# Where the weight sums of a two-level product scheme are staged and which engine makes them

## The chip, the cores and the metric

The kernel runs on one core of one Trainium2 chip. A core has a matrix engine (TensorE, PE in the profile, with its weight loads as PEld), a vector engine (VectorE, DVE), a scalar engine (ScalarE, ACT), a general engine (GpSimd, POOL) and a queue engine that issues transfers (SyncE, SP). Each engine works through its own list of instructions in order and waits at an instruction until what that instruction needs is there. ScalarE and GpSimd issue transfers too, from the same lists in which their computations stand. The metric is the device time of one execution in microseconds; of several executions the median is compared.

## The reference

The program is linear attention with a decay per head, followed by a Fourier mixing block with a two-layer network. All data are float32.

```
q, k, v: [4, 8, 768, 64]        batches, heads, rows, width of a head
per block of 64 rows:
    out   = ((q k^T) * decay mask) v + (q * lam^(i+1)) state
    state = lam^64 state + (k * lam^(63-i))^T v
x = out with the heads side by side: [4, 768, 512]
u = x + real(fft over the 768 rows and the 512 columns of x)
un = (u - mean) / sqrt(var + 1e-6)          per row
result = u + relu(un @ w1) @ w2             w1: [512, 2048], w2: [2048, 512]
```

Most of the arithmetic is in the two products with w1 and w2 over 4 x 768 = 3072 rows.

## The kernel before

**Front.** The first half of the program, up to about 420 us, goes batch by batch. Attention works in six chunks of 128 rows (`attn_in` transposes q and k on TensorE, lines 306 and 311, after loads issued in line 295; `attn_out` makes the products). The running state of attention is scaled by GpSimd in line 354 and added to by VectorE in line 355. Then `fft_ln` folds the rows and columns of the batch into sums and differences on VectorE, multiplies them with cosine and sine tables on TensorE (line 588 and lines 600 to 605) and normalises. For batches 2 and 3 the folds are made by `folds_apart`: two row blocks (128 and 65 rows), first the even folds of both (lines 507 to 516; `fe` tiles), then the odd folds (`fo` tiles). Between two of the even steps ScalarE copies one column (line 509). Rows of the mirrored half come through gathers that GpSimd issues (lines 481, 487, 494).

Four of the twelve groups of 256 rows (`PLAIN`) go through the network in plain form, woven between the front's work: line 709 makes the first layer with a relu in line 715 (VectorE) or 717 (ScalarE), line 723 the second layer, lines 734 and 735 add u, and `store` (696 on SP, 698 on GpSimd's queue) writes rows. The other eight groups write their normalised, transposed rows to DRAM (`utd`, line 652) and u to DRAM (`ud`, line 658).

**Late part.** The eight remaining groups are taken as four pairs. Each layer of a pair is computed as seven block products instead of eight (the scheme of Strassen and Winograd); in the second layer of the first pair, and in both layers of the other three (`DEEP` = 1), each of the seven is again made of seven smaller ones. `PRODUCTS` names the operands of the seven. The small products need sums of quarters of each weight operand. For product k of the first layer `block_sums` makes four sums of quarters (each 128 x 512, line 259) and writes them to DRAM (`sd`, line 261, on GpSimd's queue); `load_three` (line 836) loads three of them into `tx` tiles before every use. With `inside` true the sum number 3 replaces a quarter of the weight itself and isn't written out.

The sums of the seven products are made in three places:

- products 0, 1 and 5 in `front_sums`, by VectorE, in the second chunk of the last batch's attention, staged in tiles of the front (`ds`, `un`, two `e` tiles for each product);
- products 3 and 4 in `sums_of_first`, by VectorE, spread over the second layer of the first pair, staged in the `ur` tile that later receives the second pair's rows (`load_u`, line 825);
- products 2 and 6 in `sums_beside`, by GpSimd: product 2 when the sixth small group of the first pair's second layer begins, product 6 when the second pair's first layer begins, each with tiles of its own (`u2`).

`deep_first` (line 1043 on TensorE) makes the first layer of pairs 1 to 3 in the order `FIRST` = 0, 3, 4, 2, 1, 5, 6. `deep_second` (line 1115) makes second layers. In both, `seven` uses three PSUM banks X, Y and Z: after each small product the bank is read, and X and Z are accumulated into again by later small products, which wait for that read. The reads are ScalarE's copies (1050, 1121) where a result starts afresh, and VectorE's sums (1052, 1123) otherwise. `inputs` (872 to 899) makes the sums of the pair's rows on VectorE, and the smallest ones on GpSimd (895 to 899). `in_step` interleaves two neighbouring groups of seven, so that the last second-layer products of the first pair (1115) alternate with the first first-layer products of the second pair (1043).

**Order of the work.** The Python program is written as generators that are woven by hand; a scheduler then places each engine's instructions, and an instruction given to `tc.keep_in_program_order` holds its place among its engine's others. The order on SP's and GpSimd's queues matters as well: a transfer whose wait isn't over holds back all that stand behind it.

Of the kernel before, what the change touches and what calls it, by code (L numbers as in the profile page):

```python
# [17 lines left out]
ALU = mybir.AluOpType  # L18
# [59 lines left out]
def kernel(  # L78
# [10 lines left out]
    nc = tc.nc  # L89
    B, H, S, D = q.shape  # L90
    DM = H * D
# [8 lines left out]
    HM = DM // 2  # L100
    QM = DM // 4
    W = HM + 4
# [13 lines left out]
    def front_pool(name, bufs):  # L116
        return front_end.enter_context(tc.tile_pool(name=name, bufs=bufs, side="left"))
# [8 lines left out]
    fp = front_pool("fp", 1)  # L126
    np_ = front_pool("np", 2)
    ep = front_pool("ep", 2)
# [11 lines left out]
    def new(pool, shape, tag, **kw):  # L140
        cnt[0] += 1
        return pool.tile(shape, F32, tag=tag, name=f"{tag}{cnt[0]}", **kw)
# [46 lines left out]
    w1 = wt.tile([128, KO, DFF], F32, name="w1")  # L189
# [54 lines left out]
    def quarters_w(t):  # L244

        return [t[:, k, f:f + DFF // 4] for f in (0, DFF // 4) for k in range(2)]
# [3 lines left out]
    def block_sums(eng, queue, k, t, stage, inside, pin=tc.keep_in_program_order):  # L250

        Q11, Q12, Q21, Q22 = quarters_w(t)
        d = sums_of[k] = [dram.tile([128, DFF // 4], F32, name=f"sd{k}{i}") for i in range(4)]
        o = dict(enumerate(stage))
        if inside:
            o[3] = Q21
        for i, x, y, op in ((3, Q11, Q21, ALU.subtract), (1, Q22, 3, ALU.subtract), (0, 1, Q11, ALU.add), (2, Q12, 1, ALU.subtract)):
            x, y = (o[z] if isinstance(z, int) else z for z in (x, y))
            pin(eng.tensor_tensor(o[i], x, y, op=op))
            if i < 3 or not inside:  # L260
                queue.dma_start(d[i], o[i])
            yield 0.0

    def front_sums():

        fa, fb = slice(0, DFF // 2), slice(DFF // 2, DFF)
        for k, a in ((0, w1[:, 0:2, fa]), (1, w1[:, 2:4, fa]), (5, w1[:, 2:4, fb])):
            third = new(fp, [128, DM + 4], "ds")[:, 0:DM]
            second = new(np_, [128, DM], "un", bufs=1)
            first_, fourth = (new(ep, [128, DM], "e") for _ in range(2))  # L270
            yield from block_sums(nc.vector, nc.gpsimd, k, a, (first_, second, fourth, third), False, lambda i: i)

    xs, xn_, xd = {}, {}, {}
# [228 lines left out]
    def folds_apart(b, sets):  # L502

        tt = nc.vector.tensor_tensor
        parts = [(eo[b][a], xs[b, a][0:n], xs[b, HC + a][0:n], n) for a, n in enumerate(BLK)]
        for (e, o), lo, hi, n in parts:
            tc.keep_in_program_order(tt(e[0:n, 0, 0:DM], lo, hi, op=ALU.add))
            tt(e[0:n, 0, 1:HM], e[0:n, 0, 1:HM], e[0:n, 0, HM:DM - 1], op=ALU.add)
            nc.scalar.copy(e[0:n, :, HM:HM + 1], e[0:n, :, DM - 1:DM])
            am = e[0:n, :, W:2 * W]  # L510
            lo, hi = e[0:n, 0, 0:HM + 1], e[0:n, 1, 0:HM + 1]
            tt(am[:, 0, 0:HM + 1], lo, hi, op=ALU.add)
            tt(am[:, 1, 0:HM + 1], lo, hi, op=ALU.subtract)
            lo, hi = am[:, :, 0:QM], am[:, :, HM:QM:-1]
            tt(e[0:n, :, 0:QM], lo, hi, op=ALU.add)
            tt(e[0:n, :, QM:HM], lo, hi, op=ALU.subtract)
            yield 2.4
        for (e, o), lo, hi, n in parts:
            tc.keep_in_program_order(tt(o[0:n, 0, 0:DM], lo, hi, op=ALU.subtract))
            tt(o[0:n, 0, 1:HM], o[0:n, 0, 1:HM], o[0:n, 0, HM:DM - 1], op=ALU.subtract)  # L520
            bm = o[0:n, :, W:2 * W]
            lo, hi = o[0:n, 0, 1:HM], o[0:n, 1, 1:HM]
            tt(bm[:, 0, 1:HM], lo, hi, op=ALU.subtract)
            tt(bm[:, 1, 1:HM], lo, hi, op=ALU.add)
            lo, hi = bm[:, :, 1:QM + 1], bm[:, :, HM - 1:QM - 1:-1]
            tt(o[0:n, :, 0:QM], lo, hi, op=ALU.subtract)
            tt(o[0:n, :, QM:HM], lo, hi, op=ALU.add)
            yield 2.4
            sets.append((e, o))
        eo.pop(b)  # L530
# [215 lines left out]
    V = nc.vector  # L746
# [4 lines left out]
    s2 = Sum2()  # L751
    PRODUCTS = [("a11", "b11"), ("a12", "b21"), ("s3", "t3"), ("s2", "t2"), ("s1", "t1"), ("a22", "t4"), ("s4", "b22")]
# [48 lines left out]
    def four(*tiles):  # L801

        return [t[:, i:i + 512] for t in tiles for i in range(0, t.shape[1], 512)]
# [9 lines left out]
        for k in (3, 4):  # L813
            yield from block_sums(V, nc.gpsimd, k, s2.A[PRODUCTS[k][0]], four(ur), True)

    def sums_beside(k):

        u = [new(s2.yp, [128, G, DM], "u2", bufs=2).rearrange("p s c -> p (s c)") for _ in range(2)]
        run(block_sums(nc.gpsimd, nc.gpsimd, k, s2.A[PRODUCTS[k][0]], four(*u), True))

    def load_u(j, queue=nc.sync):

# [21 lines left out]
    DEEP = 1  # L844
# [64 lines left out]
    def load_x(j):  # L909
        P = pairs[j]  # L910
        P.us = [new(s2.yp, [128, G, DM], "u2", bufs=2) for _ in range(2)]
        for k in range(2):
            for s in range(G):
                tc.keep_in_program_order(nc.sync.dma_start(P.us[k][:, s], ud[P.who[k][s]]))
# [6 lines left out]
    def split(t):  # L921

        A11, _, A21, _ = quarters_a(t)
        tc.keep_in_program_order(V.tensor_tensor(A21, A11, A21, op=SUB))
# [105 lines left out]
    def deep_first(j, k):  # L1030

        P = pairs[j]
        h, (a, b) = P.h, PRODUCTS[FIRST[k]]
        y, fresh = (("a11", 1), ("s1", 1), ("s3", 1), ("a22", 1), ("a11", 0), ("a12", 0), ("s3", 0))[k]
        A11, A12, A3, A22 = quarters_w(s2.A[a])
        B11, T3, B21, B22 = (P.U[b][:, kt, m:m + 128] for kt in range(2) for m in (0, 128))
        (S1, S2, S4), (T1, T2, T4) = P.pre_w.pop(FIRST[k]), P.T[b]
        ab = [(A11, B11), (A12, B21), (S2, T2), (A3, T3), (S1, T1), (A22, T4), (S4, B22)]
        done = {}

        def mm(m, ps, start):
            for i in range(HF // 2):
                nc.tensor.matmul(ps[:, 128 * i:128 * i + 128], lhsT=ab[m][0][:, 128 * i:128 * i + 128], rhs=ab[m][1],  # L1043
                                 start=(start and i == 0), stop=True, skip_group_check=True)

        def read(ps, r, s, first):
            o = h[y][:, s, HF // 2 * r:HF // 2 * (r + 1)]
            p = ps.rearrange("p (a c) -> p a c", a=HF // 2)
            if first and fresh:
                nc.scalar.copy(o, p)  # L1050
            else:
                V.tensor_tensor(o, p, o, op=ADD)  # L1052
            done[r, s] = done.get((r, s), 0) + 1
            if k > 3 and done[r, s] == (1 if (r, s) == (0, 1) else 2):
                nc.scalar.activation(o, o, AF.Relu)

        if (j, k) == (DEEP, 0):
            sums_beside(6)
        yield from seven(mm, read)

        T, a11, a12, a21, a22 = (h[n] for n in ("s1", "a11", "a12", "s3", "a22"))

        def quarter_sum(o, x, y, relu=False):
            for (s, i) in ((0, 0), (0, HF // 2), (1, HF // 2), (1, 0)):
                o_, x_, y_ = (t[:, s, i:i + HF // 2] for t in (o, x, y))
                yield 0.0
                V.tensor_tensor(o_, x_, y_, op=ADD)
                if relu:
                    nc.scalar.activation(o_, o_, AF.Relu)

        if k == 1:
            yield from quarter_sum(T, T, a11)
        elif k == 2:
            yield from quarter_sum(a21, a21, T)
            load_x(j)
        elif k == 3:
            yield from quarter_sum(a12, T, a22)
            yield from quarter_sum(a22, a22, a21, True)
            yield 0.0
            split(a22)  # L1080
        elif k == 4:
            open_y(j)
            yield 0.0
            split(a11)
            yield 0.0
            yield from prepare_a(j, 0)
        elif k == 5:
            yield 0.0
            split(a12)
        elif k == 6:  # L1090
            if j + 1 < PAIRS:
                load_u(j + 1)
            yield 0.0
            split(a21)
            for s in range(G):
                yield 0.0
                V.tensor_tensor(T[:, s], a21[:, s], a22[:, s], op=ADD)

    def deep_second(j, k):

        P = pairs[j]
# [27 lines left out]
            P.reads, P.sums = 0, None  # L1129
        if j < DEEP and k == 2:  # L1130
            P.sums = sums_of_first()
        if j < DEEP and k == 5:
            sums_beside(2)
        yield from seven(mm, read, (0, 2, 3, 5, 4, 1, 6) if (j, k) == (PAIRS - 1, 6) else range(7))

        def add_u(o, y, k, m):
# [135 lines left out]
    def run(gen):  # L1272
        return sum(gen)
# [82 lines left out]
```

## Time and profile before

| what | value |
|---|---|
| median of three runs | 785.63 us (784.68 to 787.6) |
| the profiled execution, its own time | 784.18 us |
| its span in the profile | 782.3 us |
| TensorE busy, weight loads busy | 756.1 us (97%), 646.6 us (83%) |
| VectorE busy | 603.0 us (77%) |
| ScalarE busy, GpSimd busy | 231.9 us (30%), 190.5 us (24%) |
| chain that ended last | TensorE 80%, VectorE 10%, DMA 4%, issue 3% |
| DMA | 120.22 MB, mean 154 GB/s |
| granted TensorE clock | 1.00 throughout |

A row of a timeline reads: start in us, duration in us, engine, source line, operation, the tile written and the tiles read, shapes, and how many were merged. A bracket at its end gives the idle time of the engine before the row and what ended it. A row of the table of stretches gives start and end, then length, then for each engine busy time and number of instructions. Line numbers are those of the kernel before.

### The profile page before, as it was taken

To read this page: it belongs to the slowest core of one execution; us is meant where nothing else is said; L and a number is where in the kernel's file an instruction comes from. 1 tells how busy PE (TensorE), PEld (TensorE's weight loads), DVE (VectorE), ACT (ScalarE), POOL (GpSimd) and SP (SyncE) were. 2 spreads that over 40 slices of the span, in tenths; PEclk is the share of its full clock that TensorE was granted. 3 is DMA by queue.
4 is the path that set the end of the run, shared out by engine and by line. 5 is a ranking of instruction groups with operands and counts; after the bars stand their busy time and mean duration, and the time that the engine had idled before them with its cause. 6 is when DMAs were issued, how large, how long until landed. Compare 5 with 4: busy or idle time off the path is not lost.

```text
span 782.3 us, 14993 instructions
## 1 busy us (share of the span) xinstructions
PE 756.1 (97%) x5784; PEld 646.6 (83%) x5784; DVE 603.0 (77%) x1159; ACT 231.9 (30%) x532; POOL 190.5 (24%) x210
## 2 busy tenths in 40 slices
PE   6989989999999999999999999999999999999997
PEld 5768776858676876858946889999999999999997
DVE  6899889675855584546798999868986699758984
ACT  3765443325531221422101221024311342024310
POOL 3224331010102112411004961580014000230013
PEclk9999999999999999999999999999999999999999
DMA  9968723237852149721243374776545455455452
GB/s 246 266 147 233 198 95 122 90 66 206 225 144 88 54 81 211 226 96 41 55 121 106 137 241 137 272 231 198 175 136 159 148 179 176 129 183 175 138 137 77
DMA packets 152956, 120.22 MB, mean 154 GB/s; under 512 B 114238, under 2 KB 114622, under 8 KB 152886
## 3 DMA queue, kind: packets, MB, share of 16 engines
q1 hardware_dynamic: 145824, 100.51, 46.4%
q0 software_dynamic: 4032, 12.99, 4.7%
q10 hardware_dynamic: 3030, 5.78, 2.0%
q8 instruction: 46, 0.75, 0.4%
q14 instruction: 24, 0.20, 0.1%
HBM read 88.04 MB, written 31.20 MB: 152 GB/s over the span
## 4 chain that ended last, share of the span: by engine, by line
PE 80%; DVE 10%; DMA 4%; issue 3%; ACT 2%; POOL 1%; SPq 0%; DVEq 0%; POOLq 0%; ACTq 0%
PE p L1115 21%; PE p L1043 17%; PE pm L723 11%; PE pm L709 10%; PE p L959 6%; PE pa L588 3%; PE pa L330 3%; PE pa L371 3%; DMA x<-xb,ix 2%; PE pa L365 1%; PE pa L306 1%; PE pa L350 1%; DVE sc L334 1%; PE pa L311 1%; PE pa L387 1%
## 5 line engine op out<-in xcount | busy, mean ns | idle before, releaser
L709 PE MATMUL pm<-ut,w 128*128 128x256 f32 x512 | 118.7, 381 | 0.9 <-DVE hr L715 0.9
L723 PE MATMUL pm<-w,hr 128*128 128x512 f32 x256 | 115.3, 596 | 0.2 <-DVE w L228 0.2
L709 PEld LDWEIGHTS pm<-ut,w 128*128 128x128 f32 x512 | 94.4, 190 | 14.8 <-issue 2.1
L723 PEld LDWEIGHTS pm<-w,hr 128*128 128x128 f32 x256 | 46.7, 190 | 50.3 <-issue 48.7
L1138 POOL TENSOR_TENSOR y<-y,u 128x512 f32<-128x512 f32 x12 | 19.9, 1662 | 189.0 <-DVE y L1147 157.7
L1115 PE MATMUL p<-tx,sx 128*128 128x128 f32 x400 | 52.8, 275 | 1.2 <-DVE y L1123 1.2
L1115 PEld LDWEIGHTS p<-tx,sx 128*128 128x128 f32 x400 | 48.6, 192 | 1.4 <-DVE y L1123 1.4
L1052 DVE TENSOR_TENSOR ha<-p,ha 128x512 f32<-128x512 f32 x60 | 40.1, 685 | 10.0 <-PE p L1043 9.8
L302 POOL TENSOR_TENSOR kd<-k,decay 128x512 f32<-128x512 f32 x20 | 22.9, 1144 | 93.9 <-PE pa L350 51.4
L1121 ACT COPY y<-p 128x128 f32<-128x128 f32 x48 | 12.7, 266 | 103.6 <-PE p L1115 103.2
L1123 DVE TENSOR_TENSOR y<-p,y 128x128 f32<-128x128 f32 x92 | 25.6, 285 | 17.2 <-PE p L1115 10.5
L1115 PE MATMUL p<-w,ha 128*128 128x128 f32 x288 | 37.4, 275 | 0.0
L1052 DVE TENSOR_TENSOR hs<-p,hs 128x512 f32<-128x512 f32 x39 | 26.2, 684 | 14.1 <-PE p L1043 14.1
L330 PEld LDWEIGHTS pa<-qT,kT 64*128 64x128 f32 x384 | 26.1, 193 | 12.8 <-ACT qT L313 7.6
L334 DVE TENSOR_TENSOR sc<-pa,decay 128x512 f32<-128x512 f32 x48 | 31.4, 682 | 6.5 <-PE pa L330 6.2
L717 ACT ACTIVATE hr<-pm 128x256 f32<-128x256 f32 x44 | 16.7, 384 | 64.9 <-PE pm L709 64.8
L1115 PEld LDWEIGHTS p<-w,ha 128*128 128x128 f32 x288 | 34.9, 192 | 0.1
L1043 PE MATMUL p<-sx,tx 128*128 128x128 f32 x264 | 33.9, 275 | 0.0
L330 PE MATMUL pa<-qT,kT 64*128 64x128 f32 x384 | 30.7, 292 | 3.2 <-ACT qT L313 2.9
L371 PE MATMUL pa<-sc,v 128*64 128x128 f32 x384 | 29.9, 279 | 2.3 <-DVE sc L334 2.2
L621 POOL TENSOR_SCALAR ve<-mv 128x2 f32<-128x2 f32 x12 | 3.3, 278 | 117.5 <-DVE mv L618 117.5
L1043 PEld LDWEIGHTS p<-sx,tx 128*128 128x128 f32 x264 | 31.6, 192 | 0.0
(262 smaller groups left out, 1750.6 us busy)
## 6 DMA issues: line engine op xcount, KB each, us to landing
tx<-td SPq DMA_DIRECT2D x84, 256.0 KB, 2.7
raw<-in_moe_w_ch_dram SPq DMA_DIRECT2D x32, 512.0 KB, 3.6
tx<-sd SPq DMA_DIRECT2D x63, 256.0 KB, 3.0
k<-in_k_dram SPq DMA_DIRECT2D x24, 256.0 KB, 5.5
q<-in_q_dram SPq DMA_DIRECT2D x24, 256.0 KB, 5.8
v<-in_v_dram SPq DMA_DIRECT2D x24, 256.0 KB, 5.3
td<-tx SPq DMA_DIRECT2D x21, 256.0 KB, 2.2
ud<-x SPq DMA_DIRECT2D x16, 256.0 KB, 2.2
```

The lines of the kernel that those rows point to most:

```text
L302: nc.gpsimd.tensor_tensor(kd, kt, kpow, op=ALU.mult)
L330: mm(pss[hi][:, hp, :], lhsT=kT[HD[hi], hp, :], rhs=qT[HD[hi], hp, :], start=True, stop=True)
L334: nc.vector.tensor_tensor(t, pss[hi], decay[:, hi::2, :], op=ALU.mult)
L371: mm(po[HD[hi], hp, :], lhsT=vt[:, 2 * hp + hi, :], rhs=sc[hi][:, hp, :], start=(c == 0 and hp == 0), stop=(hp == HP - 1), skip_group_chec ...
L588: mm = nc.tensor.matmul(ps[:, n, :], lhsT=piece(a, i, n), rhs=cs[0:rows, a, i in (2, 3), n, :], start=(a == 0), stop=(a == 1))
L709: nc.tensor.matmul(ps, lhsT=w1[:, c, 128 * fc:128 * fc + 128], rhs=ut[:, c, :], start=(c == 0), stop=(c == KO - 1))
L723: nc.tensor.matmul(ps, lhsT=hr[(fc - f0) // 4][:, fc % 4, 128 * i:128 * i + 128], rhs=w2[:, fc, :], start=(fc == f0), stop=(fc == f1 - 1))
L959: nc.tensor.matmul(ps, lhsT=s2.A[a][:, kt, 128 * i:128 * i + 128], rhs=U[b][:, kt, :], start=(first and kt == 0), stop=(kt == 1), skip_gro ...
L1043: nc.tensor.matmul(ps[:, 128 * i:128 * i + 128], lhsT=ab[m][0][:, 128 * i:128 * i + 128], rhs=ab[m][1], start=(start and i == 0), stop=Tru ...
L1052: V.tensor_tensor(o, p, o, op=ADD)
L1115: nc.tensor.matmul(ps[:, 0:HM // 2], lhsT=ab[m][0][i], rhs=ab[m][1][:, i, :], start=(start and i == 0), stop=(i == HF // 2 - 1), skip_grou ...
L1123: V.tensor_tensor(o, ps[:, 0:HM // 2], o, op=ADD)
```

## The change

Three places are edited.

1. `front_sums` takes its twelve staging tiles at once: eight halves of the `fe` and `fo` fold tiles of both blocks, which no batch uses at that point, then `ds`, `un` and one `e` tile, and as the twelfth the first half again. The sums and their DMAs are the same.
2. `folds_apart` makes the even folds step by step over both blocks (rows, columns and the copied column of both; then the next three sums of both; then the last), with nearly all of them held in program order, and with other yields between.
3. `sums_beside` is gone. `sums_of_third` makes the sums of products 2 and 6 on VectorE, one sum after the first, second, fourth and sixth read of each of the first two first-layer products of the second pair; both products share one set of `u2` tiles, and the DMAs stay on GpSimd's queue.

```diff
     def front_sums():
 
         fa, fb = slice(0, DFF // 2), slice(DFF // 2, DFF)
-        for k, a in ((0, w1[:, 0:2, fa]), (1, w1[:, 2:4, fa]), (5, w1[:, 2:4, fb])):
-            third = new(fp, [128, DM + 4], "ds")[:, 0:DM]
-            second = new(np_, [128, DM], "un", bufs=1)
-            first_, fourth = (new(ep, [128, DM], "e") for _ in range(2))
+        idle = [new(fp, [128, 2, 2 * W], n) for n in ("fe0", "fo0", "fe1", "fo1")]
+        idle = [t[:, i, 0:DM] for t in idle for i in range(2)]
+        idle += [new(fp, [128, DM + 4], "ds")[:, 0:DM], new(np_, [128, DM], "un", bufs=1)]
+        idle += [new(ep, [128, DM], "e"), idle[0]]
+        for i, (k, a) in enumerate(((0, w1[:, 0:2, fa]), (1, w1[:, 2:4, fa]), (5, w1[:, 2:4, fb]))):
+            third, second, first_, fourth = idle[4 * i:4 * i + 4]
             yield from block_sums(nc.vector, nc.gpsimd, k, a, (first_, second, fourth, third), False, lambda i: i)
...
+        pin = tc.keep_in_program_order
         for (e, o), lo, hi, n in parts:
-            tc.keep_in_program_order(tt(e[0:n, 0, 0:DM], lo, hi, op=ALU.add))
-            tt(e[0:n, 0, 1:HM], e[0:n, 0, 1:HM], e[0:n, 0, HM:DM - 1], op=ALU.add)
+            pin(tt(e[0:n, 0, 0:DM], lo, hi, op=ALU.add))
+            pin(tt(e[0:n, 0, 1:HM], e[0:n, 0, 1:HM], e[0:n, 0, HM:DM - 1], op=ALU.add))
             nc.scalar.copy(e[0:n, :, HM:HM + 1], e[0:n, :, DM - 1:DM])
+            yield 1.0
+        for (e, o), _, _, n in parts:
             am = e[0:n, :, W:2 * W]
             lo, hi = e[0:n, 0, 0:HM + 1], e[0:n, 1, 0:HM + 1]
-            tt(am[:, 0, 0:HM + 1], lo, hi, op=ALU.add)
-            tt(am[:, 1, 0:HM + 1], lo, hi, op=ALU.subtract)
+            pin(tt(am[:, 0, 0:HM + 1], lo, hi, op=ALU.add))
+            pin(tt(am[:, 1, 0:HM + 1], lo, hi, op=ALU.subtract))
             lo, hi = am[:, :, 0:QM], am[:, :, HM:QM:-1]
-            tt(e[0:n, :, 0:QM], lo, hi, op=ALU.add)
+            pin(tt(e[0:n, :, 0:QM], lo, hi, op=ALU.add))
+            yield 1.0
+        for (e, o), _, _, n in parts:
+            am = e[0:n, :, W:2 * W]
+            lo, hi = am[:, :, 0:QM], am[:, :, HM:QM:-1]
             tt(e[0:n, :, QM:HM], lo, hi, op=ALU.subtract)
-            yield 2.4
+            yield 0.4
...
-    def sums_beside(k):
+    def sums_of_third():
 
         u = [new(s2.yp, [128, G, DM], "u2", bufs=2).rearrange("p s c -> p (s c)") for _ in range(2)]
-        run(block_sums(nc.gpsimd, nc.gpsimd, k, s2.A[PRODUCTS[k][0]], four(*u), True))
+        for k in (2, 6):
+            yield from block_sums(V, nc.gpsimd, k, s2.A[PRODUCTS[k][0]], four(*u), True)
...
             done[r, s] = done.get((r, s), 0) + 1
+            if k < 2 and sum(done.values()) in (1, 2, 4, 6):
+                next(P.sums, None)
...
-        if (j, k) == (DEEP, 0):
-            sums_beside(6)
+        if k == 0:
+            P.sums = sums_of_third() if j == DEEP else iter(())
         yield from seven(mm, read)
...
-        if j < DEEP and k == 5:
-            sums_beside(2)
```

## The prediction

> **What bounds the kernel now.** I read the page's first part, then the stretches of the span by engine, then TensorE's own timeline for every idle time in it, and last the timelines of the engines that end those idle times. TensorE is busy 756.1 of 782.3 us, so what matters is where the other 26.2 us lie. The table of stretches (us of the stretch, then busy us and instruction count of each engine, granted clock, DMA share, GB/s) says where:
>
> ```profile
> 0.00:150.00 150.00, 132.97 (x1172) 106.09 (x1173) 126.80 (x277) 73.37 (x166) 41.08 (x47) 1.00 0.68 178
> 150.00:285.00 135.00, 135.00 (x856) 98.77 (x855) 91.95 (x204) 47.79 (x109) 19.11 (x25) 1.00 0.48 124
> 285.00:320.00 35.00, 34.15 (x218) 24.07 (x219) 20.10 (x34) 7.67 (x18) 11.54 (x18) 1.00 0.74 192
> 320.00:420.00 100.00, 99.03 (x582) 69.38 (x579) 64.92 (x125) 17.73 (x48) 12.56 (x17) 1.00 0.36 99
> 507.00:513.00 6.00, 4.07 (x34) 3.69 (x34) 5.35 (x9) 0.59 (x1) 4.32 (x6) 1.00 0.86 308
> 513.00:777.00 264.00, 264.00 (x2366) 264.00 (x2366) 212.71 (x378) 68.54 (x143) 49.13 (x56) 1.00 0.52 160
> ```
>
> 17.0 us are idle before 150 us, where the change moves nothing, and 4.85 us are the tail after 777 us, where only the last stores land. Between them TensorE stands still for 0.85 + 0.97 + 0.54 + 1.93 us, and from 513 us to 777 us not at all. Its timeline names these gaps (the bracket: idle us before, and who ended it):
>
> ```profile
> 312.86 4.15 PE L709 MATMUL pm<-ut,w 128*128 128x256 f32 x18 [0.85 <-DVE hr L715]
> 361.52 1.25 PE L588 MATMUL pa<-cs,fe 65*128 65x193 f32 x6 [0.97 <-DVE fe L515]
> 508.60 1.16 PE L1115 MATMUL p<-w2s,sx 128*128 128x128 f32 x8 [0.72 <-DVE y L1123]
> 512.75 1.16 PE L1115 MATMUL p<-tx,sx 128*128 128x128 f32 x8 [1.21 <-DVE y L1123]
> ```
>
> Each of the three edits touches one of these places, and this sets the ceiling: if all four gaps closed and nothing opened, 0.85 + 0.97 + 0.72 + 1.21 = 3.75 us. Whatever else gets faster on VectorE or GpSimd is hidden behind TensorE.
>
> [...] while GpSimd computes the third sums, a 128x512 sum of VectorE takes 1.88 us and 1.23 us; afterwards, at 511.82 us, the same shape takes 0.67 us. [...] the trace has 0.67 to 0.69 us, and a start-to-start step of 0.60 us. [...]
>
> **Part 1, the front sums.** Before, the twelve VectorE sums of line 259 pass through a few staging tiles, and VectorE waits for the DMA that empties one:
>
> ```profile
> 304.05 0.69 DVE L259 TENSOR_TENSOR ds<-w 128x512 f32<-128x512 f32 x1 [4.18 <-DMA sd<-ds]
> 306.87 0.42 DVE L715 TENSOR_SCALAR hr<-pm 128x256 f32<-128x256 f32 x1 [1.52 <-PE pm L709]
> 310.33 0.69 DVE L259 TENSOR_TENSOR e<-w,un 128x512 f32<-128x512 f32 x1 [3.04 <-DMA sd<-e]
> 312.39 0.42 DVE L715 TENSOR_SCALAR hr<-pm 128x256 f32<-128x256 f32 x1
> ```
>
> The relu at 312.39 reads a bank that TensorE filled at about 310.1; behind the late sums it came 2 us late, hence the gap of 0.85 us. In the changed kernel the built order has all twelve sums in one row, before the first of these relus. From the same start, 298.45: twelve steps, nine at 0.61 and two at 0.73 where a sum needs the one just before it, plus a last 0.69 end at about 306.1. Only the eleventh waits for a DMA (it rewrites the first tile). That DMA is issued at 299.44 and, by the trace, landed by 304.0; the eleventh is due at about 304.8. So the relus come when TensorE is ready, at about 306.9 and 310.2: gain 0.85 us. Also moved: on GpSimd's queue the state scaling of line 354 (300.74 before) goes behind all twelve DMA issues, to about 308. Its reader, line 355, runs at 321.96, some 13 us of cover. The ninth to twelfth issues wait for the completion counters of the first to fourth, which land from 304 on: no cost. The burst of 3 MB meets six loads of k, q and v (300.0 to 307.6, median 5.5 us to landing); the first three land by about 309 and TensorE reads them at 316.85, so 7 us of delay are covered. Bounds: 0 to -0.85.
>
> **Part 2, the even folds.** For the last batch the path runs from a gather that lands at 355.56 through VectorE to the fold of the second block (line 515, 361.06 to 361.48), for which TensorE waits 0.97 us. In the new order that fold stands eleventh from the start at 355.75. Steps: 0.73, 0.34, 0.61, 0.34, 0.34, 0.34, 0.46, 0.34, 0.34, 0.34; it starts at about 360.2 and ends at 360.7, 0.8 us earlier, since the wait for ScalarE's one-column copy (0.26) and one dependent step are hidden. But the built order of TensorE changes here too: the half group of line 709 (0.86 us) that stood between the first matmuls and the wait now stands behind all four products. TensorE therefore gets less done while it waits: the first block's fold ends at 359.33 instead of 358.40 (0.15 us idle at 359.2), the rest goes from 360.73 to 361.98, and with the 0.86 us the same work is done at 362.84, against 362.77 before. Sum: +0.07 us, nothing. Bounds: -0.97, if the gap just closed, to +0.5. For the batch before (246.7 to 252.4) TensorE is busy with line 723 until 252.84 and its order is unchanged: nothing.
>
> **Part 3, the third and fourth sets.** Before, GpSimd computes eight sums of line 259, the first four from 502.06 to 509.8, just when VectorE prepares the second pair's inputs. GpSimd's timeline, then VectorE's:
>
> ```profile
> 502.06 1.72 POOL L259 TENSOR_TENSOR w<-w 128x512 f32<-128x512 f32 x1
> 503.86 1.60 POOL L259 TENSOR_TENSOR u<-w 128x512 f32<-128x512 f32 x1
> ```
>
> ```profile
> 507.65 0.69 DVE L872 TENSOR_TENSOR ur<-ur 128x512 f32<-128x512 f32 x1 [1.24 <-DMA ur<-utd]
> 508.26 0.28 DVE L1123 TENSOR_TENSOR y<-p,y 128x128 f32<-128x128 f32 x1
> 508.46 1.88 DVE L875 TENSOR_TENSOR sx<-ur 128x512 f32<-128x512 f32 x1
> 510.27 0.28 DVE L1123 TENSOR_TENSOR y<-p,y 128x128 f32<-128x128 f32 x1
> 510.47 1.23 DVE L877 TENSOR_TENSOR ur<-ur 128x512 f32<-128x512 f32 x1
> ...
> 512.42 0.28 DVE L1123 TENSOR_TENSOR y<-p,y 128x128 f32<-128x128 f32 x1
> ```
>
> The read at 512.42 releases TensorE at 512.75. With GpSimd idle it stands at 507.65 + 3 x (0.61 + 0.20) + 0.60 = 510.7 and ends at 511.0, before TensorE is through with its product of 510.49 (about 511.5): gain 1.21. The read at 508.26 stands behind line 872, which waits for the load of ur; that load waits for the second set's last DMA and a 5.9 us transfer, neither of which is touched: the 0.72 stays.
>
> What it adds: eight sums on VectorE, 8 x 0.60 = 4.8 us, behind line 889 (ends at about 513.1). VectorE's idle times from 515.7 to 526.5 are 1.49 + 2.46 + 0.20 + 2.71 = 6.9 us, which covers them; without that cover they'd cost up to 4.8 us. New waits: the three staged sums of the fourth set reuse the third set's tiles, so they wait for three DMAs on GpSimd's queue. There the first stands behind five small operations (0.43 each, from 513.3): issued at 515.5, landed by about 519. The second stands behind a store and line 895: issued at about 519.3, landed by about 523. The third: about 520.5 and 524. VectorE reaches the three sums at about 522, 523.5 and 527: little or no wait. Behind a waiting sum stand the reads of line 1052, for which TensorE waits if they are over some 2 us late (a bank is accumulated into again three groups of 0.89 us later). The loads of the third set on SP (520 to 527) meet the same landings, and TensorE needs them from about 531. Bounds: -1.93 to +4.8.
>
> **Sum.** -0.85 + 0.07 - 1.21 = -2.0 us on the profiled span of 782.3: 780.3. The profiled execution took 784.18, 1.9 us around the span and 1.45 under the median of 785.63. With the same 2.0 off the median: 783.6.
>
> **Rivals.** A, both gaps close: 783.6. B, only one gain arrives, because a new small wait takes the place of a gap (the burst slows the first tile's DMA, or line 889 waits for TensorE): 785.6 - 0.8 to 785.6, some 784.4 to 785.6. For it: 304.0 against 304.8 is a thin margin. Against it: neither end of it costs more than the gap of before. C, slower: VectorE blocks in the fourth set's second sum, since its tile's DMA sits on GpSimd's queue behind a store and line 895. Every us that it lands after 523.5 + 2 is a us of TensorE; the gain is used up where it lands at about 527.5, 8 us after its issue, against 2.8 to 5.3 us that the DMAs of these staged sums took between 480 and 560 us; at 10 us (529.3) the time is 783.6 + 3.8 = 787.4. D, the other gaps close as well: 785.6 - 3.75 = 781.9; against it stand the untouched load of ur and TensorE's new order. That the change does nothing needs both gaps to return, which I count with B.
>
> **How the numbers follow.** A 0.68, B 0.15, C 0.09, D 0.08. The range 781.7 to 786.4 takes in A with about 1 us of scatter of a median (the three runs spread by 2.9), B, D, and the mild end of C; outside remain the rest of C and scatter. Within 0.5% (3.9 us, about what a measurement of this kernel can tell from no change) means 781.7 to 789.6: A, B and most of D, 0.84. Faster takes scatter on D and A, 0.10; slower the long end of C, 0.06.
>
> **What would show it.** Right: no idle time at line 709 near 312 us; twelve line-259 sums within 8 us; no gap before the product that stood at 512.75, one of about 0.7 before its predecessor at 508.60; VectorE's sums of lines 875 and 877 at 0.7 us; no idle time on TensorE from there to 777. In the even folds a gap of about 1.2 us instead of 0.97. Wrong: VectorE idle behind a DMA of u in the second pair's first layer, or behind a sum at 305 us, with TensorE idle after it; transposes of line 306 waiting for k.

## The result and the profile after

| what | before | after |
|---|---|---|
| median | 786.4 us (784.68 to 787.87) | 784.06 us (782.04 to 788.57) |
| ratio of the times, 95% interval | | 0.9976 [0.9966, 0.9987], that is -1.9 us |
| the profiled execution, its own time | 784.18 us | 782.96 us |
| its span | 782.3 us | 780.7 us |
| VectorE busy, GpSimd busy | 603.0 us, 190.5 us | 600.9 us, 181.9 us |

The medians are of 22 runs each, taken side by side. The gain of 0.24% is small, but its interval doesn't reach 1. VectorE took over eight sums and is nevertheless busy for less time: sums that took 1.88 and 1.23 us now take 0.68 and 0.97.

Line numbers have moved: 709, 715, 723, 588, 515, 1115, 1123, 1043 and 1052 of before are 718, 724, 732, 597, 520, 1127, 1135, 1053 and 1062 after; lines 872, 875 and 877 are 882, 885 and 887, and 895 is 905. Lines 259 and 261 stayed.

The table of stretches of the changed kernel (us of the stretch, then busy us and instruction count of TensorE, its weight loads, VectorE, ScalarE and GpSimd, granted clock, DMA share, GB/s):

```profile
285.00:320.00 35.00, 35.00 (x238) 25.15 (x238) 19.09 (x36) 7.66 (x18) 11.96 (x19) 1.00 0.78 216
507.00:513.00 6.00, 4.82 (x43) 4.63 (x42) 5.51 (x13) 0.58 (x1) 1.69 (x2) 1.00 0.52 183
513.00:777.00 264.00, 262.81 (x2354) 262.62 (x2352) 216.07 (x383) 68.55 (x143) 46.98 (x54) 1.00 0.52 163
```

From 285 to 320 us TensorE no longer stands still. From 507 to 513 us it has 1.18 us idle instead of 1.93, and GpSimd 1.69 us of work instead of 4.32. The 1.19 us missing at the very end are no gap: TensorE ends earlier.

TensorE's timeline of the changed kernel, first around the even folds of the last batch, then the one gap at the change of pairs (the bracket: idle us before, and who ended it):

```profile
351.31 7.07 PE L718 MATMUL pm<-ut,w 128*128 128x256 f32 x32
358.71 0.59 PE L597 MATMUL pa<-cs,fe 128*128 128x193 f32 x2 [0.33 <-DVE fe L520]
360.05 1.25 PE L597 MATMUL pa<-cs,fe 65*128 65x193 f32 x6 [0.74 <-DVE fe L520]
361.14 1.89 PE L718 MATMUL pm<-ut,w 128*128 128x256 f32 x8
362.86 1.48 PE L597 MATMUL pa<-cs,fe 128*128 128x193 f32 x8
...
508.44 1.16 PE L1127 MATMUL p<-w2s,sx 128*128 128x128 f32 x8 [1.18 <-DVE y L1135]
```

The gap at 312 us is gone. One gap in the folds has become two, and the half group of line 718 stands behind all the products that wait, where before half of it ran ahead of the wait. At the change of pairs one of two gaps is left, and it is longer: 1.18 instead of 0.72 us.

VectorE's timeline of the changed kernel, at the end of the twelve front sums and at the change of pairs:

```profile
305.46 0.68 DVE L259 TENSOR_TENSOR e<-un,w 128x512 f32<-128x512 f32 x1
307.01 0.42 DVE L724 TENSOR_SCALAR hr<-pm 128x256 f32<-128x256 f32 x1 [0.86 <-PE pm L718]
310.46 0.42 DVE L724 TENSOR_SCALAR hr<-pm 128x256 f32<-128x256 f32 x1 [3.03 <-PE pm L718]
...
507.49 0.69 DVE L882 TENSOR_TENSOR ur<-ur 128x512 f32<-128x512 f32 x1 [3.31 <-DMA ur<-utd]
508.30 0.68 DVE L885 TENSOR_TENSOR sx<-ur 128x512 f32<-128x512 f32 x1
509.10 0.97 DVE L887 TENSOR_TENSOR ur<-ur 128x512 f32<-128x512 f32 x1
```

The relus now wait for TensorE, where TensorE waited for a relu. The input sums of lines 885 and 887 take 0.68 and 0.97 us instead of 1.88 and 1.23.

**A ledger.** Brackets are only part of the account. The same TensorE instruction can be looked up in both profiles, and how much earlier it starts tells what has been won so far:

| TensorE instruction | before | after | difference | what lies between it and the row above |
|---|---|---|---|---|
| line 371 / 373, beside the first front sum | 298.70 | 298.84 | +0.14 | start of the program, scatter |
| line 723 / 732, second layer of a plain group | 348.86 | 347.87 | -0.99 | front sums: -1.13 |
| line 588 / 597, first product after the even folds | 363.48 | 362.86 | -0.62 | folds: +0.37 |
| line 1115 / 1127, last product before the wait for `ur` | 506.82 | 506.20 | -0.62 | nothing |
| line 1115 / 1127, first product after it | 508.60 | 508.44 | -0.16 | wait for the load of `ur`: +0.46 |
| line 1043 / 1053, the product behind the second gap's | 513.75 | 512.12 | -1.63 | third set: -1.47 |
| end of the span | 782.3 | 780.7 | -1.6 | nothing more |

### The profile page after: what moved, and what is told of

Same layout as the page of the kernel before. It is cut to its first block, busy times and chain, and to the rows that moved or that the text cites. A ratio compares the mean times of both kernels' runs of the same rounds, so it can differ in the third digit from the quotient of the medians.

```text
span 780.7 us, 14995 instructions
## 1 busy us (share of the span) xinstructions
PE 756.3 (97%) x5784; PEld 646.9 (83%) x5784; DVE 600.9 (77%) x1167; ACT 231.9 (30%) x532; POOL 181.9 (23%) x202
## 4 chain that ended last, share of the span: by engine, by line
PE 85%; DVE 7%; DMA 4%; ACT 2%; issue 1%; POOL 1%; DVEq 0%; ACTq 0%; POOLq 0%
PE p L1127 22%; PE p L1053 17%; PE pm L732 12%; PE pm L718 11%; PE p L969 6%; PE pa L597 3%; PE pa L332 3%; PE pa L373 3%; PE pa L367 2%; DMA x<-xb,ix 2%; PE pa L308 1%; PE pa L352 1%; PE pa L313 1%; PE pa L389 1%; DVE sc L336 1%
## 5 line engine op out<-in xcount | busy, mean ns | idle before, releaser
L319 DVE TENSOR_TENSOR qs<-pa,qpow 128x512 f32<-128x512 f32 x20 | 13.7, 686 | 24.3 <-ACT qT L315 24.2
```

## The experiments

All ratios are to the kernel before, run beside each kernel on the same chip, with 95% intervals; a thousandth is about 0.8 us. There were three series of runs: the first four kernels; e5 to e8; and e9 to e12. Each kernel also left one profile.

The theory is that of the prediction: three separate effects, the front sums no longer ahead of a relu, the folds reordered for nothing, and, at the change of pairs, GpSimd's third-set sums no longer beside VectorE's input sums. The rivals are that the gain is one of the parts alone, and, for the third set, that it comes from something else that moved with it: the writes of the sums, or the fourth set.

**One part at a time.** Three kernels with one edit each, and one with edits 1 and 3:

```diff
 e1_front: edit 1 alone
+        idle = [new(fp, [128, 2, 2 * W], n) for n in ("fe0", "fo0", "fe1", "fo1")]
...
 e2_folds: edit 2 alone
+            pin(tt(am[:, 0, 0:HM + 1], lo, hi, op=ALU.add))
...
 e3_third: edit 3 alone
-    def sums_beside(k):
+    def sums_of_third():
...
 e4_front_third: edits 1 and 3
```

> Only the front sums' staging is changed. Theory (the gap of 0.85 us before line 709 near 312 us came from relus standing behind VectorE sums that waited for a staging tile's DMA): the gap is gone, the rest of TensorE's gaps stay as before (0.97, 0.72, 1.21), and the time is 0.9 to 1.1 us below the kernel before, ratio about 0.9987. Rival (the twelve DMAs in a row slow the loads of k, q and v, so that the gap comes back at the transposes of line 306): a new gap between 312 and 325 us, ratio 1.000 or above.

> Only the even folds' order is changed. Theory (VectorE's fold of the second block comes about 0.8 us earlier, but TensorE's half group of line 709, 0.86 us, moves behind the wait and the first block's fold comes 0.9 us later): two gaps near 359 and 361 us of 1.0 to 1.2 us together, the whole 0.1 to 0.4 us slower than before, ratio about 1.0003. Rival (the gap just shrinks by what VectorE gains): one gap under 0.3 us, ratio about 0.999.

> Only the third and fourth sets of sums move to VectorE. Theory [...]: the gap of 1.21 us at 512.75 is gone, the one of 0.72 before it stays between 0.5 and 1.2, VectorE's two slow sums (1.88 and 1.23 us) take 0.7 to 1.0; the time is 0.9 to 1.4 us below before, ratio about 0.9985. Rival (VectorE's new waits for the staged tiles' DMAs give it back): idle time of VectorE behind a DMA of u after 520 us and gaps on TensorE after it, ratio 1.000 or above.

> The change without its part on the even folds. Theory (the three places add up, and the folds' part costs a little): 2.0 to 2.4 us below before and 0.1 to 0.4 us below the changed kernel, ratio about 0.9972. Rival (the folds' part brings part of the changed kernel's gain): 1.0 to 1.6 us below before, above the changed kernel.

| kernel | median us | ratio |
|---|---|---|
| e1_front | 786.83 | 0.9986 [0.9969, 1.0003] |
| e2_folds | 788.96 | 1.0007 [0.9983, 1.0030] |
| e3_third | 786.06 | 0.9973 [0.9958, 0.9988] |
| e4_front_third | 784.67 | 0.9968 [0.9951, 0.9984] |

The order is as forecast: the front gains about 1.1 us (its interval takes in 1), edit 3 gains 2.1 us, more than the 0.9 to 1.4 expected, and no gain or loss of the folds can be told. e1_front has no idle time at the transposes either, so the burst of DMAs did not slow the loads that they wait for by enough to show. In each profile the gaps go where their edit goes: without edit 1 the gap of line 709 is there (0.89 and 1.02 us), with it there is none; with edit 3 there is a single gap at the change of pairs. The surprise is in the two kernels that keep the third set on GpSimd. Their gaps at the change of pairs look unlike those of before. First GpSimd's and VectorE's timelines in e1_front, each in its own fence, then TensorE's:

```profile
508.04 1.28 POOL L259 TENSOR_TENSOR u<-w,u 128x512 f32<-128x512 f32 x1
```

```profile
507.59 2.28 DVE L874 TENSOR_TENSOR ur<-ur 128x512 f32<-128x512 f32 x1 [1.64 <-DMA ur<-utd]
```

```profile
510.13 1.16 PE L1117 MATMUL p<-w2s,sx 128*128 128x128 f32 x8 [2.70 <-DVE y L1125]
```

Here GpSimd's sum fell on the first of the input sums (line 872 of before, 874 here; 0.69 us before) and not on the second and third, so the loss sits in one gap of 2.70 us instead of two that add to 1.93. In e2_folds it fell on the same sum (2.18 us) and the gap is 2.71 us, but something followed it. TensorE's timeline in e2_folds, then its table of stretches, and last that of e1_front:

```profile
512.61 2.08 PE L1122 MATMUL p<-w2s,sx 128*128 128x128 f32 x8 [2.71 <-DVE y L1130]
```

```profile
508.00:510.00 2.00, 1.90 (x17) 1.71 (x16) 0.32 (x2) 0.00 (x0) 1.68 (x3) 1.00 0.98 340
510.00:512.00 2.00, 0.00 (x0) 0.00 (x0) 1.82 (x1) 0.00 (x0) 1.78 (x2) 1.00 0.94 238
512.00:514.00 2.00, 1.39 (x6) 1.39 (x7) 2.00 (x5) 0.00 (x0) 1.01 (x2) 0.64 0.94 353
514.00:516.00 2.00, 2.00 (x12) 2.00 (x11) 2.00 (x7) 0.00 (x0) 1.23 (x1) 0.51 0.21 83
516.00:518.00 2.00, 2.00 (x20) 2.00 (x20) 0.84 (x3) 0.58 (x1) 0.00 (x0) 1.00 0.70 262
```

```profile
506.00:508.00 2.00, 1.43 (x13) 1.23 (x12) 0.41 (x1) 0.00 (x0) 1.70 (x2) 1.00 1.00 328
508.00:510.00 2.00, 0.00 (x0) 0.00 (x0) 2.00 (x3) 0.00 (x0) 1.68 (x3) 1.00 0.81 154
510.00:512.00 2.00, 1.87 (x16) 1.87 (x17) 2.00 (x6) 0.00 (x0) 0.63 (x2) 1.00 0.92 366
512.00:514.00 2.00, 2.00 (x20) 2.00 (x19) 2.00 (x5) 0.59 (x1) 1.24 (x1) 1.00 0.10 41
```

Eight matmuls take 2.08 us instead of 1.16, at a granted clock of 0.64 and then 0.51; from 516 to 518 us it is 1.00 again. After the equally long gap of e1_front the clock stayed at 1.00, though the stretches at the two gaps are much alike: 1.90 us of TensorE's work and then none in e2_folds, 1.43 and then none in e1_front. So a fall of the clock can follow on a gap of 2.7 us; what decides whether it does isn't shown. The fall cost 1.58 us: from its first product behind the gap to the product after the next one e2_folds takes 3.47 us and e1_front 1.89.

**What the third set does.** The changed kernel again, beside one that puts only the third set back on GpSimd at its old place (the fourth stays on VectorE), and two that leave the change as it is but let GpSimd add idle sums at the old place, four and five of 128 x 512. They go into spare tiles that nobody reads, without any DMA: if GpSimd's sums slow VectorE's input sums by running beside them, these do too.

```diff
 e10_third_back, against the changed kernel
-        for k in (2, 6):
+        for k in (6,):
...
+        if j < DEEP and k == 5:
...
+            run(block_sums(nc.gpsimd, nc.gpsimd, 2, s2.A[PRODUCTS[2][0]], four(*u), True))
 e5_lock_back (spare), e9_lock_five (spare + spare[:1])
...
+            for o in spare + spare[:1]:
+                tc.keep_in_program_order(nc.gpsimd.tensor_tensor(o, Q[0], Q[1], op=SUB))
```

> The changed kernel again, on the chip of the three runs beside it, to compare them with. Theory: gaps of 0.3 and 0.7 us at the folds, one of 1.0 to 1.3 us before the first product that waits for the load of ur, no slow input sum, ratio to before 0.997 to 0.9985.

> The changed kernel with the third set (product 2) back on GpSimd at its old place, the fourth set (product 6) still on VectorE. Theory (the collision of the third set with VectorE's input sums is the whole loss): the slow input sums and gaps of 1.9 to 2.9 us are back, 0.8 to 2.2 us slower than the changed kernel beside it. Rival (the fourth set on GpSimd was the loss): as the changed kernel.

> The changed kernel, and in it four sums of GpSimd (128x512, two inputs from the weights, written to spare tiles that nobody reads) where the third set stood before. Theory [...]: one of VectorE's first three input sums takes 1.5 to 2.3 us again, TensorE's gaps there grow from 1.18 to 1.9 to 2.9 us, and the kernel is 0.8 to 2.2 us slower than the changed one, ratio to before about 0.999. Rival (the gain is the order of GpSimd's queue or fewer DMAs): the gaps stay at 1.0 to 1.2 us and the time is that of the changed kernel.

> As the run with four idle sums of GpSimd, but with five, so that GpSimd computes for about 7.9 us from about 500 us on, as long as the third set with its DMAs took before (7.7), and is still busy when the load of ur lands. Theory [...]: one of the first three input sums (lines 882, 885, 887) takes 1.2 to 2.3 us, TensorE's gaps there are 1.9 to 2.9 us, 0.8 to 2.2 us slower than the changed kernel run beside it. Rival (GpSimd's DMAs and its queue were the cause): as the changed kernel, gaps 1.0 to 1.3.

| kernel | median us | ratio |
|---|---|---|
| e12_after_again | 784.73 | 0.9972 [0.9955, 0.9988] |
| e10_third_back | 787.1 | 0.9997 [0.9982, 1.0012] |
| e9_lock_five | 786.75 | 0.9981 [0.9965, 0.9998] |
| e5_lock_back (in another series) | 785.51 | 0.9985 [0.9962, 1.0009] |

With the third set back, the whole gain of edit 3 is gone: 0.0025, or 2.0 us, against 2.1 us when edit 3 was made alone. The two intervals overlap by 0.0006, and e3_third says the same from the other side with an interval clear of 1. The fourth set can stay on VectorE without being felt, so the third set is the cause. VectorE's timeline in e10_third_back, GpSimd's, and TensorE's:

```profile
510.94 2.04 DVE L885 TENSOR_TENSOR sx<-ur 128x512 f32<-128x512 f32 x1
513.10 1.23 DVE L887 TENSOR_TENSOR ur<-ur 128x512 f32<-128x512 f32 x1
```

```profile
511.13 1.29 POOL L259 TENSOR_TENSOR u<-w,u 128x512 f32<-128x512 f32 x1
```

```profile
511.07 1.16 PE L1127 MATMUL p<-w2s,sx 128*128 128x128 f32 x8 [0.55 <-DVE y L1135]
515.39 1.16 PE L1127 MATMUL p<-tx,sx 128*128 128x128 f32 x8 [1.37 <-DVE y L1135]
```

That is the picture of before, row by row: a sum of about 2 us, one of 1.23 us, and the second gap.

The idle sums were to say whether GpSimd's arithmetic alone does it, without the writes. With four of them the experiment missed: GpSimd ran from 508.41 to 514.69 us in that profile and `ur` landed at 514.3, so that only the tail of the last idle sum met an input sum: line 882 took 0.93 instead of 0.69 us, and a single gap of 1.27 us remained. It says little about the cause, and its time isn't told from that of the changed kernel. With five, the last one meets two input sums. GpSimd's timeline in e9_lock_five, first merged and then from 509.82 us on, where the last idle sum alone is in view, then VectorE's and TensorE's:

```profile
503.51 8.05 POOL L1148 TENSOR_TENSOR u<-w 128x512 f32<-128x512 f32 x5
```

```profile
509.77 1.80 POOL L1148 TENSOR_TENSOR u<-w 128x512 f32<-128x512 f32 x1
```

```profile
510.56 1.55 DVE L885 TENSOR_TENSOR sx<-ur 128x512 f32<-128x512 f32 x1
```

```profile
514.25 1.16 PE L1127 MATMUL p<-tx,sx 128*128 128x128 f32 x8 [0.61 <-DVE y L1135]
```

The sum of line 885 takes 1.55 instead of 0.68 us and the second gap is back, without one transfer. So arithmetic on GpSimd is enough to open it. In the times the size is unclear: the ratios of e9_lock_five and e12_after_again lie 0.7 us apart, with intervals that overlap, and the medians 2.0 us. That arithmetic alone makes up the full 2.0 us isn't shown. What the writes of the third set add, if anything, stays open.

**Giving the folds cover.** In the folds TensorE runs out of work. Line 580 of before, 589 after (the pause that `fft_ln` yields after the folds, in units of the work that is woven in) decides how much of a plain group stands ahead of the first product that waits. Longer by 1.7 for the last batch only, once on the changed kernel and once with edits 1 and 3 and the old folds:

```diff
-            yield 12.0 if b - 1 in LEADS else 9.0
+            yield 12.0 if b - 1 in LEADS else 10.7 if b == B - 1 else 9.0
```

> The changed kernel with one number altered: after the last batch's folds 10.7 is yielded in place of 9.0, which puts one more group of the plain first layer (four products, 1.73 us) on TensorE ahead of the first product that needs a fold. Theory (what the folds' part costs or brings is decided by how much of TensorE's work stands ahead of the wait): the gaps of 0.33 and 0.74 us are gone and nothing opens later, 1.0 to 1.5 us below the changed kernel, ratio to before about 0.996. Rival (the group is only moved, and its place later in the batch's transforms becomes a gap, since the copies of the transforms' results wait): the gap comes again between 362 and 385 us, time as the changed kernel.

> The change without its folds' part (old order of the even folds), with 10.7 yielded after the last batch's folds. Theory (TensorE's work ahead of the wait decides, and the new order of the folds brings only what VectorE gains, 0.8 us): in the built order five groups of the plain layer stand ahead of the folds' products; the second block's fold ends some 9.2 us after TensorE enters them and 8.65 us of work stand there, so one gap of 0.3 to 0.7 us stays; 0.3 to 0.7 us slower than the changed kernel with the same 10.7. Rival (the new order is needed for the cover to work): a gap of over 1 us stays.

e7_cover took 783.66 us, 0.9951 [0.9938, 0.9964]; e11_cover_old_folds 783.67 us, 0.9949 [0.9929, 0.9969]. Against the changed kernel's 0.9976 and 0.9972 that is some 2 us less, where 1.0 to 1.5 had been expected, and the times show no difference between the two orders of the folds once there is cover. TensorE's timeline in e7_cover, there and where the late part begins, then in e11_cover_old_folds:

```profile
354.43 8.80 PE L718 MATMUL pm<-ut,w 128*128 128x256 f32 x40
363.06 1.48 PE L597 MATMUL pa<-cs,fe 128*128 128x193 f32 x8
364.37 1.89 PE L718 MATMUL pm<-ut,w 128*128 128x256 f32 x8
...
423.02 1.10 PE L969 MATMUL p<-sx,w1s 128*128 128x256 f32 x4 [1.02 <-DVE sx L872]
```

```profile
352.27 8.80 PE L711 MATMUL pm<-ut,w 128*128 128x256 f32 x40
360.91 1.88 PE L590 MATMUL pa<-cs,fe 128*128 128x193 f32 x8
362.63 1.89 PE L711 MATMUL pm<-ut,w 128*128 128x256 f32 x8
```

The rows of the folds give their price at this place, because the same 40 matmuls of line 718 and 8 of line 597 stand in all four kernels. In e7_cover they go from 354.43 to 364.37, in 9.94 us, with no wait at all. In e11_cover_old_folds they take 10.36, so 0.42 us are lost inside the group of eight, though no gap is listed (0.3 to 0.7 us had been expected as a listed gap). In the changed kernel they take 362.86 - 351.31 = 11.55, a loss of 1.61; in the kernel before, 363.48 - 352.29 = 11.19, a loss of 1.25. So the new order costs 0.36 us more than the old one where there is no cover, and with cover 0.42 us less, which didn't reach the times. The cover isn't free: the work moved ahead is missing later, and the gap at the beginning of the late part, 0.54 us before and after, is 1.02 us in e7_cover and 1.03 in e11_cover_old_folds. That nothing would open later was wrong by this half us.

**Loading the second pair earlier.** The gap that edit 3 leaves waits for the load of `ur`, and that load waits until the second set of sums, staged in the same tile, has been written out: in the kernel before it stood on SP's queue for that for 4.8 us. Starting these sums one product earlier, on edits 1 and 3, and then together with the cover on the whole change:

```diff
-        if j < DEEP and k == 2:
+        if j < DEEP and k == 1:
             P.sums = sums_of_first()
```

> The change without its folds' part, and the first pair's sums for products 3 and 4 begin one product earlier, so that the tile that they are staged in comes free earlier. Theory (the gap of about 1.1 us before the product that stood at 508.6 is the load of ur, which waits for the second set's last DMA): the load is issued 3 to 6 us earlier, the gap is gone, about 1.1 us below the run without the folds' part, ratio to before about 0.995. Rival (the load waits for something else on SP's queue, or VectorE is so full in that stretch that its reads come late): the gap stays or new ones open between 470 and 500 us, ratio 0.997 or above.

> The changed kernel with both alterations, the earlier first sums and the 10.7. Theory: TensorE has no gap of over 0.6 us between 150 and 776 us; 2.0 to 2.6 us below the changed kernel, ratio to before about 0.9945. Rival (the two don't add, since the stall of one moves into the other's place): 1.0 to 1.5 us below the changed kernel.

e6_first_k1 took 784.08 us, 0.9966 [0.9949, 0.9982], against 0.9968 without the edit, in another series: no gain that can be told, where about 1.1 us had been expected. In its profile the gap shrank from 1.09 to 0.34 us, but less than the head start: the last write of a sum was issued at 492.90 and landed only at about 500.0, and SP's queue stood for it, so the load of `ur` left at 500.16 and 501.48 us.

e8_all took 782.48 us, 0.9944 [0.9926, 0.9961]: 4.4 us faster than the kernel before. Against the kernel as changed, whose ratio is 0.9976 in one series and 0.9972 in another, it lies 2 to 3 us lower. There `ur` was loaded from 495.82 us and the gap at the change of pairs is gone; the gap of 1.02 us at 420.16, where the late part begins, is the only one of over 0.6 us from 150 to 776 us.

## Why the prediction was right, step by step

**The total.** 783.6 us were predicted and 784.06 measured; -2.0 us against -1.9 in the ratio and -1.6 in the span. The medians lie 2.3 us apart; 783.6 was counted from an earlier median of 785.63. It is rival A, both gaps closed. That the total fits so closely is luck in part. Four terms were off: the front by -0.28, the folds by +0.30, the wait for `ur` by +0.46 and the third set by -0.26 us, and these errors nearly cancel.

**Part 1, front sums: mechanism right, size too small.** The sums end at 306.14 (forecast 306.1), the relus run at 307.01 and 310.46 (forecast 306.9 and 310.2), the state scaling at 308.32 (forecast 308), behind a twelfth issue that waited 0.58 us for the landing of an earlier one. None of the twelve sums waits for a tile at the end of the row, which the thin margin of 304.0 against 304.8 had left in doubt, and the transposes of k begin at 315.87 us without a wait. The term was put at -0.85; the ledger has -1.13 and e1_front timed -1.1. It was mis-sized by taking the bracket of the gap for its cost (below).

**Part 2, even folds: the mechanism right, one arrival left out.** The forecast saw that the half group of line 709 goes behind the wait and that the shorter chain on VectorE pays nothing, and set +0.07; the cost is +0.37. The term that failed is that chain. It has the second block's rows there when they are wanted, at 355.75 + 0.73 + 0.34 = 356.82 us. But the gather that brings them (line 494, issued at 353.76) landed at 357.06 in the trace of before. Nothing waited for it there, since VectorE came to these rows only at 358.65. In the new order VectorE waits; its timeline in the changed kernel:

```profile
356.16 0.69 DVE L510 TENSOR_TENSOR fe<-x,x 65x512 f32<-65x512 f32 x1 [0.22 <-DMA x<-xb,ix]
```

All eight profiles with the new order have this wait, of 0.20 to 0.40 us. On the clock of before (the folds' first row on TensorE starts at 352.29 there and 0.98 us earlier in the changed kernel) the second block's fold ends at 360.97 instead of 360.7, and TensorE goes on at 361.03 instead of 360.73. These 0.30 us are the difference between +0.07 and +0.37. A slip of the prediction that did no harm: its ten steps add up to 359.93, not to the 360.2 that it goes on with; one more step of 0.34 would give that, and in the trace eleven stand ahead of the fold. Told by the gaps, it is the same: a loss of 1.25 us with one bracket of 0.97 before, and of 1.61 with two that add to 1.07 after. In the times the part isn't told from nothing (1.0007 [0.9983, 1.0030]).

**Part 3, third and fourth sets: mechanism right, size too small, and not one number.** The forecast had the sums of lines 875 and 877 at 0.7 us and the second gap gone, -1.21, again the bracket taken for the cost. They are 0.68 and 0.97 us, the gap is gone, and the ledger has -1.47. The 0.97 shows a small misreading: in the kernel before, line 877 did not meet the third set, whose last sum ended at 509.79, but a sum of 128 x 128 that stays on GpSimd (line 897, 0.47 us from 510.67; line 907 after, 0.45 us from 509.07). In the times edit 3 is worth 2.0 to 2.1 us. What was missed is that one profile shows one draw of the collision. Idle time of TensorE at the change of pairs, in the profiles that leave the load of `ur` as it was:

| third set on | kernel: idle us at the change of pairs (of it, by the load of `ur` alone) |
|---|---|
| GpSimd | before 1.93 (0.72), e10_third_back 1.92 (0.44), e1_front 2.70 (1.11), e2_folds 2.71 (1.23) and then a lowered clock |
| VectorE | e3_third 1.03, e4_front_third 1.09, after 1.18, e11_cover_old_folds 1.21, e7_cover 1.59, e12_after_again 1.76 |

The load's part can be taken off: in the second row the idle time is always 0.10 to 0.12 us less than the time from the start of TensorE's last product before the wait to VectorE's first input sum, and the same difference gives the numbers in brackets. What remains for the collision is 1.21, 1.48, 1.59 and 1.48 us, 1.44 in the mean. An estimate from these four profiles: with 0.27 us for the second gap that two of them have, and the 1.58 us of one fall of the clock, it comes to 2.0 us a run, or 1.6 without the fall. Four profiles are few, and how often the clock falls there isn't known. Nor is it known whether it is chance that the load came 0.4 us later in the mean of the second row.

**The 0.72 that was to stay** stayed in kind: line 872 / 882 still waits for the load of `ur`, before and after. Its size did not. It went to 1.18 us, since the load landed later in relation to TensorE, and to 1.76 in e12_after_again, the same kernel, where 1.0 to 1.3 had been expected and VectorE waited 3.90 us for it, against 3.31. It is a transfer's landing that varied between two profiles of one kernel; "neither of which is touched" was true and no reason for it to be the same number.

**The rivals.** Rival C, VectorE blocked behind a DMA of `u`, did not come. The DMAs of the third set went out at 516.36, 519.69 and 521.10 (forecast 515.5, 519.3, 520.5), the eight sums begin between 513.19 and 527.43 us, none of them waits for a DMA, and TensorE has no gap there. The idle time of VectorE did cover them. Rival B would need a new wait in place of a gap; there is none at 312 nor at 512 us. Rival D, that all gaps close, needed other edits: e8_all, with more cover and an earlier load, comes near it.

## What to carry over

When a kernel is bound by TensorE, compare the start of the same TensorE instruction in two profiles, and don't add up the idle brackets: each gap here cost about 0.27 us more than it lists, so the order that split one wait in two lost 1.61 us against 1.25, though the listed sum rose only from 0.97 to 1.07. Put the work that can cover a wait ahead of it first; here 1.7 units more of woven work were worth more than either order of the folds, though half a us of it came back as a gap later. When an order lets an engine come to its rows earlier, look up when they land. And keep GpSimd's 128x512 sums away from VectorE sums on which TensorE waits: here a VectorE sum of 0.69 us took 1.55 to 2.28 us beside one. What that costs depends on which sum is hit and on the clock, so one profile shows one draw of it.

## What was not expected of the hardware

**A VectorE sum that GpSimd stops ends about 0.55 us after GpSimd's sum, and the starts in a profile don't always tell who stops whom.** In e1_front VectorE's sum begins at 507.59 and GpSimd's 0.45 us later, at 508.04, and yet VectorE is stopped: GpSimd's ends at 509.32, VectorE's at 509.87, 0.55 later. In e10_third_back the four times are 510.94, 511.13, 512.42 and 512.98. In both, GpSimd's sum follows at once on its issue of a DMA (line 261, in e1_front from 507.46 us). Whether this decides it isn't tested; behind another such issue, of 519.69 us in the changed kernel, VectorE's sum of 520.14 kept its 0.69 us and GpSimd's small one of 520.26 took 0.88. Where GpSimd had been idle, the sum of VectorE that began first kept its time and GpSimd's took longer. VectorE's timeline in the changed kernel, then GpSimd's:

```profile
513.19 0.68 DVE L259 TENSOR_TENSOR w<-w 128x512 f32<-128x512 f32 x1
```

```profile
513.35 0.83 POOL L907 TENSOR_TENSOR sv<-sx 128x128 f32<-128x128 f32 x1 [1.56 <-DVE sx L899]
```

The small sum of line 907 takes 0.45 us at 509.07. In e9_lock_five both happen in a row: line 882 begins at 509.75, keeps its 0.69 us, and the idle sum that begins at 509.77 takes 1.80 instead of 1.26; line 885 begins at 510.56, inside that sum, and ends at 512.11, 0.55 us after it. GpSimd's spans in a profile are rough, but the same distance returns in the kernel before (lines 875 and 877: 0.55 and 0.56 us), in e2_folds (0.56) and in e5_lock_back (0.56). A reading of these numbers, not tested by itself, is that VectorE then has most of its 0.69 us of work still to do.

**An idle bracket leaves out about 0.27 us of what a gap costs TensorE**, by the rows of the folds: 1.25 against 0.97 with one gap, 1.61 against 1.07 with two. The front gap points the same way (1.13 against 0.85), and the third set's (1.47 against 1.21). The rows at the change of pairs show where it goes. A row of eight matmuls lasts 1.06 us but the next one starts after 0.89, so 0.17 us of a row's end, which is modelled, lie under the next row where there is no gap. And the first row behind a gap takes 1.00 us to the next one's start, 0.11 more.

**About half the clock followed on one gap of 2.7 us and not on another.** In e2_folds the clock is 0.64 and 0.51 in the two stretches from 512 to 516 us, behind a gap of 2.71 us; in e1_front it is 1.00 in every stretch from 506 to 516 us, around a gap of 2.70. At the end of the span longer idle times leave it as it is for a while: in the kernel before TensorE's last product ends at 777.45 us and the clock is 1.00 up to 782; in the changed kernel it ends at 775.82, and the clock is 1.00 up to 780 us and 0.63 in the last 0.7 us. The mean clock of the profiled execution is 0.994 to 0.998 in six of the fourteen profiles (e2_folds, e3_third, e4_front_third, e5_lock_back, e7_cover and e10_third_back) and 0.999 or 1.00 in the others. When the clock falls isn't explained by these; no run varied it on purpose.
